# A gated attention and feed-forward kernel: the first loads cut into smaller pieces, and the instruction order made anew

## The chip, the cores and the metric

The kernel runs on one core of a Trainium2 chip. The metric is the time of the whole launch on the device in microseconds (us). The median of three runs of the kernel before is 235.07 us, the lowest 234.68 and the highest 235.65. Lower is better.

## The reference, cut to what matters

One input `x` of 2048 tokens by 512 features goes through two branches, and a gate per token mixes them:

```
g = sigmoid((x * gate_w).sum(-1))
qkv = x @ wqkv                         # 32 heads of 16
scores = q @ k.T * 16**-0.5            # key within the last 256 tokens, causal
a = (softmax(scores) @ v) @ wo
b = (silu(x @ w1) * (x @ w3)) @ w2     # 512 -> 1376 -> 512
out = g * a + (1 - g) * b
```

All inputs and the output are bf16. TensorE accumulates in f32.

## The kernel before, in words

Everything stays in SBUF. The tokens are worked on in four chunks of 512 (called `tq` in the attention branch and `tcb` in the feed-forward branch), and the heads in four groups of eight (called `c`). `xT` holds x transposed, features on the partitions. Its first chunk is made on TensorE: `load_x` (line 394) brings rows of x into `xs`, four tiles of 128 tokens; line 493 transposes each tile with four matmuls against the identity; lines 498 (VectorE) and 500 (ScalarE, tile 2 only) copy the result into `xT`. The other three chunks are made by DMA transposes, four for each chunk (`turn_x`, line 399).

Work on TensorE, by line of the profile: 420 is warm-up, matmuls of constants that nothing reads; 493 is the transposes; 553 is the products for q and k, 606 the ones for v; 661 (main) and 711 (edge) are the scores; 801 is the mix of the probabilities with v; 904 is a few columns left over by the feed-forward branch and the gate; 967 is the products with w1 and w3 for a block `f` of 128 hidden columns; 1026 and 1082 are the products with w2; 1055 is the product with wo. Line 665 and line 715 on ScalarE are the exponentials of the scores (60 main and 16 edge groups). Lines 977, 981 and 987 make the hidden block from the products of line 967.

Three forms of matmul use the array differently. Most products use all 128 rows and 128 columns ("full"). The scores use 32 rows at a time, four matmuls beside each other ("row"). The mix of line 801 uses 17 columns at a time, four beside each other ("column").

The order is made by a planner in the kernel itself, run when the program is built. `add` notes an operation with its engine, a duration, what it depends on, and a due time; `Plan.emit` is a list scheduler that goes through a model of the engines and picks, among the operations that could start, the one with the earliest due time. It charges 0.108 us (`SWITCH`) where TensorE goes from one form to another. Each engine then runs its instructions in exactly that order, and waits at one that is not ready. Due times come from formulas with the constants of the dictionary `K`, plus a correction for each operation out of the list `SHIFT` (1518 numbers). Two constants weigh forms: `ADJ` makes a score or mix group more urgent when TensorE is already out of the full form, `SEP` moves the due time of a mix group when it is in the full form. The list `landed` tells the planner when loads arrive.

`opening()` runs ahead of the planner's order: constants on GpSimd, `warm_up(WARM)` on TensorE, and then the loads, in the order written, on the queues of SyncE (SP) and ScalarE (ACT). `load_w(..., True)` splits a load of weights into two halves of the contraction, one on each queue; without `True` it goes on SP alone. The loads on SP after the first columns of w1 are: the first columns of k's weights, of w3, of q's weights, of v's weights, then the middle columns of w1 and of w3 (line 406 all of them), then the DMA transposes of the second chunk (line 399), with the remaining columns of w1 and w3 and the transposes of the third chunk behind them.

For the first chunk the first products don't wait for all of x: the block `f = 0` with w1, and q and k, are made in two halves of 256 tokens, so that the first half needs x tiles 0 and 1 only. In the block `f = 1` the four matmuls have 512 tokens each, and in the planner's model they wait for the block before them, its product with w3 included (`last_up`).

Of the kernel before, what the change touches and what calls it, by code (L numbers as in the profile page):

```python
# [21 lines left out]
    0, 0, 0, 0, 0, 0, 0, 0, 0, 0, 0, 0, 0, 0, 0, 0, 0, 143.67, 103.37, 60.03, 88, 142.21, 38.94, 42.12, -2.51, 57.41,  # L22
    7.18, 5.57, 21.6, 47.86, 56.17, 15.18, 29.67, -86.47, 13.05, -39.24, 93.68, 44.01, 89.92, -46.77, -6.15, 204.82,
    244.36, 118.35, -0.3, 95.3, 208.67, 25.01, 209.9, 27.11, 36.54, -10.95, -9.39, 52.09, 0.17, 72.67, 71.83, 128.25,
    6.95, 43.72, 49, 19.26, 15.62, -14.34, -2.54, -2.99, -55.81, 62.72, 81.66, -59.72, 182.92, 1.14, 47.94, -51.05,
    34.34, 120.64, -10.49, -37.49, -6.12, 109.58, 7.32, 0.8, 2.54, 4.2, -2.85, -45.95, -9.51, -2.95, -20.63, 0.64,
    1.17, 35.64, 39.39, 131.17, 8.36, 8.93, 28.12, 5.47, 64.98, 117.35, 1.82, 6.71, 27.65, -126.55, -12.59, -19.75,
    3.38, -14.15, 36.7, 31.02, 55.28, -21.94, 5.71, -3.9, 18.93, 47.83, 4.25, 248.79, -3.85, 44.01, 54.86, -56.69,
    127.59, -36.08, 122.73, 149.98, 17.63, -69.18, 35.62, 91.79, 17.07, 187.88, 62.3, -10.76, 56.83, 74.21, 98.54,
    100.73, -24.69, -15.4, -41.78, -18.37, 109.81, -34.23, 179.41, 88.53, 19.81, -33.97, 126.03, 79.32, 23.61,  # L30
    -111.17, 187.19, 73.42, -15.39, -4.02, 168.01, -6.39, 2.63, -49.27, -6.51, -21.07, -10.37, 98.77, -31.22, 26.94,
    -14.53, -25.32, -4.69, 10.73, -3.69, -10.22, -23.5, 6.07, 21.26, -12.87, -9.95, 66.48, 12.55, 19.01, -14.97,
    -12.27, 17.42, -5.66, 54.92, -7.76, 5.66, 29.85, 3.41, -8.01, 102.45, 40.82, 70.9, 23.07, 49.07, -36.02, 39.67,
    -10.85, -93.98, -13.12, -39.31, -4.37, 22.32, 105.78, -4.03, -8.06, -27.45, 9.46, 252.7, 20.84, -42.23, 96.29,
    107.25, -16.6, 28.68, -10.33, -22.99, 40.24, 29.98, 93.7, -5.71, 5.47, 151, 208.74, 26.61, -42.84, 51.17, -52.39,
    104.04, 21.6, 119.61, 49.37, 6.4, 83.87, 72.92, -18.55, 258.45, 169.05, 39.53, 6.4, 30.89, 29.41, 36.06, -22.79,
    40.5, 30.01, 194.39, 106.93, 198.49, 59.17, 15.42, -22.13, 31.91, -121.23, -43.1, -47.51, 37.94, 50.7, 26.07,
    -32.38, 33.8, 28.69, 14.17, 9.66, -86.66, -8.77, 15.07, 50.34, -64.11, -3.44, 7.45, -67.78, 110.17, -63.05,
    -178.58, 2.13, 121.36, -21.41, -44.26, 16.75, -37.15, -40.61, -95.25, -94.71, -87.05, -24.61, 13.42, -59.78,
    -67.44, 41.44, -101.56, 11.06, -33.11, -71.21, -28.85, 104.6, 24.33, -40.69, -52.39, -9.63, 26.77, -100.79,  # L40
    -90.72, -16.71, -49.95, 0.77, 56.94, 31.08, 2.94, 85.99, -47.92, -4.21, -10.14, -49.68, -59.14, -20.47, 17.05,
    9.18, -136.81, -17.89, -31.18, -53.9, -51.12, -31.87, -117.82, -45.29, -37.28, -12.19, -1.25, 41.48, -13.15,
    -2.78, -20.58, 70.46, -9.65, 0.42, -7.8, 138.5, 3.14, -40.82, -3.62, -15.69, -66.41, -68.61, 48.26, 0.27, -16.69,
    -84.28, 9.7, 64.3, 5.27, -19.71, -2.32, 46.57, -29.07, 2.28, -87.36, -30.22, -9.39, 9.35, -12.6, 137.81, -7.54,
    -44.64, -15.97, -33.95, 39.77, -67.24, -102.54, -33.51, 16.97, 33.23, -20.98, 103.26, -74.1, -20.35, -129.81,
    -11.87, 70.04, -37.92, -31.23, -31.72, 115.18, -5.02, 7.08, -36.32, -89.83, 69.39, -21.91, -127.54, -91.99, 58.96,
    47.44, 24.28, -21.24, -24.84, 6.43, -17.59, 13.95, 53.11, -173.96, -3.2, 2.87, 76.58, -23.35, 0.24, 44.93, 6.77,
    32.61, -43.31, -3.8, 54.69, 32.74, 20.67, -11.12, -7.84, -5.91, 113.99, 8.97, 31.35, 9.04, -33.31, -70.77, 125.18,
    -11.8, 13.25, 41.86, -23.6, 32.12, -117.51, -69.74, 4.45, 3.22, -45.12, -13.56, 7.83, -1.49, -61.88, -17.3,
    -30.07, 81.28, 54.45, 60.43, 3.73, 8.99, -19.3, -55.65, -126.93, 28.33, -26.47, -99.46, -105.24, -53.49, -36.19,  # L50
    -105.94, -6.28, -8.53, 9.04, -131.6, -67.07, -32.86, -0.62, -26.8, -15.17, 42.29, -25.61, 0.66, -115.05, 8.73,
    -156.43, -126.84, -74.33, -116.11, -42.3, 106.05, -83.79, -84.91, -56.93, -39.89, 40.69, -58.82, -16.3, -68.75,
    -113.67, -46.33, -55.59, 86.72, -2.31, -4.54, -147.15, -65.61, -56.93, -9.05, -63.33, -74.13, -51.4, -43.18,
    -165.22, -18.68, 28, 28.73, -49.15, -97.68, -110.31, -7.88, -19.74, 90.28, -107.22, 10.84, -11.65, -12.48,
    -139.53, 101.05, 15.07, 40.93, -29.49, -17.58, -11.49, -93.56, -20.27, -15.93, 1.59, -20.21, -55.65, -25.66,
    -13.61, -2.96, 15.71, -29.74, -54.27, -59.15, -10.64, -38.16, -50.35, 98.06, 69.37, -37.63, -5.15, -141.83,
    165.05, -222.91, 67.89, -61.75, -90.82, 86.05, 60.99, -103.98, -18.7, 43.14, 47.89, -10.91, -25.67, -47.43, 11.14,
    8.9, 37.39, -55.89, -46.72, -5.35, 19.74, -95.65, -21.88, -53.61, -8.14, -32.99, -73.67, -20.88, 10.04, -67.08,
    143.23, 72.28, 2.19, 196.98, -84.67, -76.21, -83.98, 32.86, -106.11, -80.37, -10.73, 2.47, -154.03, -73.23, 83.93,
    4.83, -11.7, 18.76, 4.53, -5.17, -169.97, -86.68, 36.64, 7.28, -109.75, -129.22, 9.09, -37.03, -73.61, -50.85,  # L60
    -82.09, 34.51, -83.71, -84.57, -105.55, -51.2, -28.08, -96.33, 16.35, -21.62, -35.06, -64.78, 140.85, -38.85,
    -76.38, -48.32, 0.11, -136.54, -65.55, -85.88, -68.18, -1.47, -19.95, -104.98, 3.42, -38.57, -97.15, -46.27,
    27.73, 19.45, -81.04, -136.13, -59.96, -160.69, -114.6, -45.93, 209.18, 10.81, -66.32, -51.02, -128.13, 16.41,
    -129.46, -42.8, 69.77, -11.72, -85.17, -0.02, 13.79, 51.92, -164.37, -35.41, -17.3, 107.06, -55.49, -146.53,
    13.95, -10.84, -8.11, -173.24, -84.51, 51.45, -6.56, -9.72, -138.28, -139.48, -56.4, -80.09, -20.29, -124.07,
    -28.97, -198.75, -2.49, 31.49, -109.38, 49.16, -19.84, -90.85, -183.08, 86.7, -11.55, 75.95, -47.51, -13.11,
    -143.48, -132.62, -156.14, -139.7, -162.81, -118.44, 35.58, -10.76, -13.59, -122.48, -167.03, -145.19, -108.13,
    1.53, -98.19, -90.01, -124.36, 4.22, -3.94, -76.47, 44.12, 1.73, -108.31, -4.23, -120.54, 3.35, -9.5, 1.03, -2.62,
    5.39, -177.73, -56.91, -103.65, -64.6, -98.27, -76.43, -36.83, -179.23, -130.6, -147.17, 84.55, -107.32, 11.46,
    -3.2, -25.91, 22.58, -171, -129.24, -77.58, 13.67, 4.85, -93.34, -179.61, -36.75, 1.36, 26.22, -125.29, -138.89,  # L70
    -153.86, 5.16, -51.58, -76.87, -154.65, 16.68, -60.17, 17.84, -81.88, -0.77, -11.98, -199.53, -3.2, 24.53,
    -122.57, -80.18, -107.59, 21.59, 22.98, -80.5, -145.36, -152.67, 31.99, -91.15, -114.97, 76.44, 30.12, -168.03,
    -152.87, -62.63, -31.09, -23.28, 1.02, 10.23, 23.56, -68.32, -141.82, -74.89, -41.69, 2.78, -111.71, -179.08,
    19.29, -12.38, -129.45, -108.99, -87.66, -25.52, -79.85, 86.01, -135.14, 135.58, -177.44, -51.77, -30.02, -113.8,
    40.25, 16.46, -216.88, -6.71, 16.72, 10.99, 0.28, 36.46, 16.66, 21.49, 86.9, -7.91, -4.28, -35.85, 116.8, 116.67,
    -6.87, 31.59, -21.27, 46.82, -51.08, -6.69, -18.61, 1.49, 62.93, 119.51, 65.71, -24.1, 3.72, -24.61, -20.61,
    -63.52, 73.67, 28.77, 35.06, 50.97, -44.06, 2.71, -54.72, -37.79, -0.52, 55.39, -42.49, -33.84, -34.29, -35.32,
    5.43, 14.68, 19.8, -12.27, 83.28, 73.04, 16.23, -39.95, 12.12, -46.08, 10.28, -22.12, 11.92, 209.9, 5, 0.32,
    66.04, -19.2, 12.74, -42.84, 22.8, 5.12, 159.56, 0.64, 41.85, -25.48, 72.07, 125.81, 95.22, 36.82, 36.62, 10.6,
# [183 lines left out]
def kernel(  # L263
# [12 lines left out]
    nc = tc.nc  # L276
# [17 lines left out]
    VW = DH + 1  # L294
    HALF = (0, 1, 2, 3, 4)
    SCALE = float(DH) ** -0.5
    WARM = 30

    pp = ctx.enter_context(tc.tile_pool(name="pp", bufs=1))
    ps = ctx.enter_context(tc.tile_pool(name="ps", bufs=1, space=bass.MemoryType.PSUM))  # L300
# [148 lines left out]
    T0, TA, TF0, TF1 = K["T0"], K["TA"], K["TF0"], K["TF1"]  # L449
# [684 lines left out]
```

## Time and profile before

| what | value |
|---|---|
| median of 3 runs | 235.07 us (234.68 to 235.65) |
| the profiled execution's own time | 235.33 us |
| its span, first to last instruction | 233.6 us |
| PE (TensorE) busy | 225.2 us, 96% of the span |
| ScalarE, VectorE, GpSimd busy | 181.9, 181.7, 152.8 us |
| read from HBM, written | 6.85 MB, 2.10 MB |

The profiled execution took 1.7 us more than its span, which is what lies before the first and after the last instruction. Busy time of PE is not PE at its peak: the durations of matmuls overlap, so the stretches in which the array streams nothing are found from the starts of the instructions, not from the busy share.

### The profile page before, as it was taken

To read this page: it belongs to the slowest core of one execution; us is meant where nothing else is said; L and a number is where in the kernel's file an instruction comes from. 1 tells how busy PE (TensorE), PEld (TensorE's weight loads), DVE (VectorE), ACT (ScalarE), POOL (GpSimd) and SP (SyncE) were. 2 spreads that over 40 slices of the span, in tenths; PEclk is the share of its full clock that TensorE was granted. 3 is DMA by queue.
4 is the path that set the end of the run, shared out by engine and by line. 5 is a ranking of instruction groups with operands and counts; after the bars stand their busy time and mean duration, and the time that the engine had idled before them with its cause. 6 is when DMAs were issued, how large, how long until landed. Compare 5 with 4: busy or idle time off the path is not lost.

```text
span 233.6 us, 8254 instructions
## 1 busy us (share of the span) xinstructions
PE 225.2 (96%) x3596; PEld 115.9 (50%) x3635; DVE 181.7 (78%) x317; ACT 181.9 (78%) x165; POOL 152.8 (65%) x245
## 2 busy tenths in 40 slices
PE   7999999999999999999999999999999999999995
PEld 7545545634544345545547353535444355455543
DVE  5457777993798869987878787887986779997864
ACT  3479999797778998878998989887968998867310
POOL 7135999576877964749865869567679856654300
DMA  6997701800004000000003000000000000140202
GB/s 188 322 183 196 93 1 21 225 27 1 6 4 133 3 11 14 3 3 3 4 12 81 25 1 3 3 3 0 4 3 3 0 3 18 34 145 20 91 7 84
DMA packets 20653, 11.57 MB, mean 50 GB/s; under 512 B 10025, under 2 KB 20617, under 8 KB 20617
## 3 DMA queue, kind: packets, MB, share of 16 engines
q1 hardware_dynamic: 19920, 10.62, 19.5%
q8 instruction: 28, 0.46, 0.8%
q10 hardware_dynamic: 696, 0.43, 0.6%
q14 instruction: 9, 0.07, 0.1%
HBM read 6.85 MB, written 2.10 MB: 38 GB/s over the span
## 4 chain that ended last, share of the span: by engine, by line
PE 89%; DMA 4%; SPq 2%; issue 2%; DVE 2%
PE ch L967 30%; PE ch L1026 16%; PE ch L553 11%; PE ch L801 9%; PE su L661 8%; PE ch L606 6%; PE ch L1055 6%; PE su L711 2%; DMA xT<-in_A_x_dram 2%; SPq L399 2%; DMA xs<-in_A_x_dram 2%; PE ch L1082 1%; PE ch L904 1%; SPq L406 1%; DVE bsb L1030 0%
## 5 line engine op out<-in xcount | busy, mean ns | idle before, releaser
L665 ACT ACTIVATE Em<-su 128x2048 bf16<-128x2048 f32 x60 | 112.7, 1878 | 22.5 <-PE su L661 20.9
L967 PE MATMUL ch<-xT,w_sb 128*128 128x512 bf16 (+1 forms) x304 | 77.0, 377 | 2.7 <-issue 1.7
L675 POOL TENSOR_SCALAR_AFFINE_SELECT Em<-Em 64x512 bf16<-64x512 bf16 x56 | 37.8, 674 | 26.2 <-ACT Em L665 24.5
L670 POOL TENSOR_SCALAR_AFFINE_SELECT Em<-Em 64x512 bf16<-64x512 bf16 x60 | 40.5, 676 | 18.0 <-ACT Em L665 16.0
L728 POOL TENSOR_SCALAR_AFFINE_SELECT Ee<-Ee 64x1024 bf16<-64x1024 bf16 x32 | 39.5, 1233 | 11.4 <-ACT Ee L715 10.3
L967 PEld LDWEIGHTS <-w_sb 128*128 128x128 bf16 x324 | 28.7, 98 | 32.8 <-issue 4.7
L981 DVE SCALAR_TENSOR_TENSOR h<-tt,ch 128x512 bf16<-128x512 bf16 (+1 forms) x44 | 29.7, 679 | 12.9 <-ACT tt L977 12.6
L1026 PE MATMUL ch<-w_sb,hT 128*128 128x512 bf16 x143 | 37.0, 380 | 0.8 <-issue 0.6
L553 PE MATMUL ch<-xT,wqkv_sb 128*128 128x512 bf16 (+1 forms) x126 | 33.5, 367 | 0.6 <-issue 0.3
L715 ACT ACTIVATE Ee<-su 128x2048 bf16<-128x2048 f32 x16 | 30.1, 1880 | 5.0 <-PE su L711 5.0
L642 POOL COPY vs<-vs 64x256 bf16<-64x256 bf16 x64 | 28.9, 452 | 7.5 <-DVE vs L630 3.1
L987 DVE SCALAR_TENSOR_TENSOR hT<-h,ch 128x512 bf16<-128x512 bf16 x40 | 27.1, 682 | 5.4 <-PE ch L967 3.3
L977 ACT ACTIVATE tt<-ch 128x512 bf16<-128x512 f32 (+1 forms) x44 | 26.1, 598 | 3.9 <-PE ch L967 3.1
L801 PEld LDWEIGHTS <-vs 128*17 128x17 bf16 x1664 | 20.5, 92 | 5.8 <-issue 4.5
L801 PE MATMUL ch<-Em,vs 128*17 128x256 bf16 (+2 forms) x672 | 22.6, 242 | 0.0
L801 PE MATMUL ch<-Ee,vs 128*17 128x64 bf16 x992 | 22.1, 193 | 0.0
L1026 PEld LDWEIGHTS <-hT 128*128 128x128 bf16 x150 | 13.5, 98 | 16.4 <-issue 2.5
L553 PEld LDWEIGHTS <-wqkv_sb 128*128 128x128 bf16 x136 | 12.0, 97 | 13.3 <-issue 2.7
L606 PE MATMUL ch<-wqkv_sb,xT 128*128 128x256 bf16 x128 | 17.2, 273 | 0.2 <-issue 0.2
L661 PE MATMUL su<-qT,kz 32*128 32x256 bf16 x240 | 17.3, 278 | 0.0
L661 PE MATMUL su<-qT,k 32*128 32x256 bf16 x240 | 16.6, 268 | 0.0
L661 PEld LDWEIGHTS <-kz 32*128 32x128 bf16 x240 | 6.0, 91 | 21.2 <-issue 20.8
(83 smaller groups left out, 251.9 us busy)
## 6 DMA issues: line engine op xcount, KB each, us to landing
out_dram<-ot SPq DMA_DIRECT2D x15, 128.0 KB, 1.7
wqkv_sb<-in_A_wqkv_dram SPq DMA_DIRECT2D x6, 256.0 KB, 4.5
w_sb<-in_B_w_dram SPq DMA_DIRECT2D x2, 608.0 KB, 4.8
w_sb<-in_B_w_dram SPq DMA_DIRECT2D x3, 384.0 KB, 3.8
w_sb<-in_B_w_dram SPq DMA_DIRECT2D x2, 512.0 KB, 6.5
wo_sb<-in_A_wo_dram SPq DMA_DIRECT2D x4, 128.0 KB, 3.2
xs<-in_A_x_dram ACTq DMA_DIRECT2D x1, 256.0 KB, 3.8
xs<-in_A_x_dram SPq DMA_DIRECT2D x1, 256.0 KB, 3.5
```

The lines of the kernel that those rows point to most:

```text
L553: nc.tensor.matmul(pst[:, t0:t1], lhsT=wqkv_sb[:, dc, col + c * P:col + (c + 1) * P], rhs=xT[:, dc, tq * 512 + t0:tq * 512 + t1], start=(d ...
L606: nc.tensor.matmul(ch[vj.at["ch"]][:, (m - m0) * 2 * P:(m - m0 + 1) * 2 * P], lhsT=xT[:, dc, m * P:(m + 1) * P], rhs=wqkv_sb[:, dc, 2 * D ...
L661: nc.tensor.matmul(su[:, s, a * 256:(a + 1) * 256], lhsT=head_keys(r, t, a), rhs=qT[r, q0:q0 + 256], start=True, stop=True)
L665: nc.scalar.activation(out=Em[job.at["Em"]][:], in_=su[:].rearrange("p s (a q) -> p s a q", a=2), func=ACT.Exp, scale=SCALE)
L670: nc.gpsimd.affine_select(out=e, in_=e, pattern=[[0, 8], [1, KB]], compare_op=ALU.is_ge, fill=0.0, base=0, channel_multiplier=-1)
L675: nc.gpsimd.affine_select(out=e, in_=e, pattern=[[0, 8], [-1, KB]], compare_op=ALU.is_ge, fill=0.0, base=-1, channel_multiplier=1)
L715: nc.scalar.activation(out=Ee[ej.at["Ee"]][:].rearrange("p s t k q -> p s (t k q)"), in_=su[:], func=ACT.Exp, scale=SCALE)
L728: nc.gpsimd.affine_select(out=e, in_=e, pattern=[[0, 4], [0, 4], [1, KB]], compare_op=ALU.is_ge, fill=0.0, base=0, channel_multiplier=-1)
L801: nc.tensor.matmul(po[32 * s:32 * s + VW, lo - 512 * w:hi - 512 * w], lhsT=vs[:, i, a * VW:(a + 1) * VW], rhs=mov, start=(n == 0), stop=(n ...
L967: nc.tensor.matmul(ch[job.at["ch"]][:, t0:t1], lhsT=wA[:, dc, :] if joint else w[:, dc, f * P:(f + 1) * P], rhs=xT[:, dc, tcb * 512 + t0:t ...
L981: nc.vector.scalar_tensor_tensor(out=h1[job.at["h1"]][ru, :], in0=tt[job.at["tt"]][rg, :], scalar=1.0, in1=ch[job.at["ch"]][rg, :], op0=AL ...
L1026: nc.tensor.matmul(bps[:], lhsT=ht[:, mm * P:(mm + 1) * P], rhs=w2_sb[0:fs, f, :], start=(f == 0), stop=(f == NFC - 1))
```

## The change

The loads of x are cut from two pieces of 256 KB into four of 128 KB, one for each tile of 128 tokens. Tiles 0 and 1 go first, one on each queue; then come the two halves of w1's first columns; then tiles 2 and 3. The warm-up has 23 matmuls where it had 30. For the first chunk the product of w1 with block `f = 1` is made in two halves of 256 tokens, as block `f = 0` was already, and the planner no longer makes it wait for `last_up`. `landed` has new arrival times for x and for w1's first columns. The constants `K` are new, and so are all numbers of `SHIFT` (now 1516, since two operations are gone); with them the order of the whole program is a new one. The numbers of `SHIFT` are cut here to the first line of each list.

```diff
 SHIFT = [
-    0, 0, 0, 0, 0, 0, 0, 0, 0, 0, 0, 0, 0, 0, 0, 0, 0, 143.67, 103.37, 60.03, 88, 142.21, 38.94, 42.12, -2.51, 57.41,
...
+    0, 0, 0, 0, 0, 0, 0, 0, 0, 0, 0, 0, 0, 0, 0, 0, 0, 4.69, -2.58, -20.58, -2.83, 1.06, 0.72, 24.53, 0.21, 7.18,
...
 ]
-    WARM = 30
+    WARM = 23
-    K = {"T0": 1.021, "TA": 175.674, "TF0": -5.614, "TF1": 219.201, "PV": -22.302, "EDGE": -2.04, "HOLD": -6.16, "LEAD": -1.713, "QLEAD": -2.523, "V": 9.16, "O0": 9.293, "O1": -5.39, "O2": 6.658, "O3": 32.037, "FE": 0.855, "PE": 8.645, "VE": -2.133, "MK": 65.837, "UP": 4.276, "_km": 1.0, "_lo": 1.0, "LE": 1.877, "ADJ": 7.677, "SEP": -19.643, "BE": 5.555, "OE": 1.299, "END": 5.842}
+    K = {"T0": 2.227, "TA": 175.361, "TF0": -4.255, "TF1": 213.877, "PV": -6.113, "EDGE": 0.732, "HOLD": -0.443, "LEAD": 0.942, "QLEAD": -5.414, "V": 7.151, "O0": 14.885, "O1": 5.66, "O2": 8.135, "O3": 27.069, "FE": 2.213, "PE": 8.461, "VE": -3.49, "MK": 40.302, "UP": 6.634, "_km": 1.0, "_lo": 1.0, "LE": -1.709, "ADJ": 2.616, "SEP": -4.351, "BE": 8.777, "OE": 3.124, "END": 7.045}
@@ opening()
         warm_up(WARM)
 
-        load_x(0, 2, nc.sync)
-        load_x(2, 4, nc.scalar)
+        load_x(0, 1, nc.sync)
+        load_x(1, 2, nc.scalar)
         load_w(w1_sb, B_w1, 0, 2 * P, True)
+        load_x(2, 3, nc.sync)
+        load_x(3, 4, nc.scalar)
         nc.scalar.activation(out=gt[:, 0:4], in_=nc.const_aps.tensor_like(1.0, gt[:, 0:4]), func=ACT.Tanh)
         nc.scalar.dma_start(out=gwr[:], in_=gate_w.rearrange("(c p) -> c p", p=P))
         load_w(wqkv_sb, A_wqkv, D, D + 2 * P)
@@ arrivals
-    landed = {"x": [3.6, 3.6, 4.4, 4.4, 14.5, 20.6], "w13": [5.25, 7.45, 10.8, 16.6, 12.2, 18.8],
+    landed = {"x": [3.25, 3.6, 5.4, 5.6, 14.5, 20.8], "w13": [4.8, 7.45, 10.8, 16.6, 12.2, 18.8],
               "qkv": [6.5, 8.3, 9.1], "gw": 8.0}
@@ feed-forward, block f of chunk tcb
-            if tcb or f:
+            if tcb or f > 1:
                 a = plan.pieces(HALF, 0.2155, lambda lo, hi, half=half, job=job: half(job, w1_sb, lo, hi),
                                 xt_ready[tcb] + win + last_up + (w_ab if joint else []), due, [(job, "ch")])
             else:
                 (two halves of 256 tokens, the second behind x tiles 2 and 3)
```

## The prediction

> **What bounds the kernel now.** I read the page first, then the busy time by stretches.
>
> ```profile
> PE 225.2 (96%) x3596; PEld 115.9 (50%) x3635; DVE 181.7 (78%) x317; ACT 181.9 (78%) x165; POOL 152.8 (65%) x245
> PE 89%; DMA 4%; SPq 2%; issue 2%; DVE 2%
> 18.00:70.00 52.00, 51.10 (x873) 26.81 (x885) 40.18 (x71) 43.95 (x42) 40.25 (x67) 1.00 0.27 62
> ...
> 180.00:225.00 45.00, 44.31 (x770) 21.65 (x776) 38.14 (x63) 31.66 (x27) 24.96 (x32) 1.00 0.13 40
> ```
>
> TensorE (PE) is the bound: 89% of the chain that ended last is its work, and from 18 to 225 us it idles about 1 us in 50. The other engines have a fifth of their time free. So a change to the order can help in three ways only: by an earlier start of dense PE work, by less PE time that streams nothing, or by a shorter tail. The tail first, out of the chain of waits:
>
> ```profile
> 228.96 1.84 PE ch L1082 x22
> 230.82 0.35 DVE ot L1086
> ```
>
> After the last matmul (230.79) come one eviction and one store, to 233.6: 2.8 us that no edit touches but the order. I take 0 for it.
>
> Which PE time streams nothing? The chain of waits, in two places, and the counts of score groups on the page:
>
> ```profile
> 17.42 0.65 PE ch L553 x3
> 18.07 0.33 PE su L661 x8
> 18.40 0.32 PE ch L553
> ...
> 36.70 0.33 PE su L661 x8
> 37.03 1.12 PE ch L801 x80
> 38.15 0.32 PE ch L967
> ...
> 208.44 1.46 PE ch L801 x112
> 209.90 0.33 PE su L661 x8
> L665 ACT ACTIVATE Em<-su 128x2048 bf16<-128x2048 f32 x60 | 112.7, 1878 | 22.5 <-PE su L661 20.9
> L715 ACT ACTIVATE Ee<-su 128x2048 bf16<-128x2048 f32 x16 | 30.1, 1880 | 5.0 <-PE su L711 5.0
> ```
>
> A matmul of 512 columns takes 0.65 / 3 = 0.216 us in a row of its kind; after a score group the next takes 0.32. So each change of form, into the score form or out of it, costs 0.32 - 0.216 = about 0.11 us. There are 60 + 16 = 76 score groups and, counted along PE's order, 17 mix groups (line 801). Each alone between full matmuls would mean 2 x 93 = 186 changes. Where a mix group touches a score group, one change is saved. That is so in 14 places (the first at 36.70, the last at 209.90), so there are 172 changes, 172 x 0.11 = 18.9 us. This is the one large item that a new order can move.
>
> **The opening, as it stands.** Engine by engine in order of time, PE alone:
>
> ```profile
> 0.85 3.17 PE L420 MATMUL su<-const-bfloat16-1.0 128*128 128x128 bf16 x30 [0.85 <-PEq L1118]
> 4.34 0.62 PE L493 MATMUL ch<-ident,xs 128*128 128x128 bf16 x8 [0.31 <-DMA xs<-in_A_x_dram]
> 4.91 0.61 PE L493 MATMUL ch<-ident,xs 128*128 128x128 bf16 x8
> 5.58 1.07 PE L967 MATMUL ch<-xT,w_sb 128*128 128x256 bf16 x8
> 6.80 1.04 PE L553 MATMUL ch<-xT,wqkv_sb 128*128 128x256 bf16 x8 [0.15 <-issue]
> 15.31 1.03 PE L553 MATMUL ch<-xT,wqkv_sb 128*128 128x512 bf16 x3
> ```
>
> and the durations of single instructions by line (shortest, median, longest in ns), the third of the lines from 4 to 8 us:
>
> ```profile
> L420 PE MATMUL su<-const-bfloat16-1.0 x32: 219/311/311, 0.9 to 4.9; 128*128 128x128 bf16 x32
> L493 PE MATMUL ch<-ident,xs x16: 217/219/229, 4.3 to 5.3; 128*128 128x128 bf16 x16
> L967 PE MATMUL ch<-xT,w_sb x10: 270/272/379, 5.6 to 7.9; 128*128 128x256 bf16 x8, 128*128 128x512 bf16 x2
> ```
>
> Useful PE work begins at 4.34 with the transposes. Real products begin at 5.58. The eight half-width matmuls from 5.58 take 1.07 - 0.27 (the last one's own duration) over seven steps, 0.11 each, so they stream until 5.58 + 8 x 0.11 = 6.46; the next work waits for k's weights and starts at 6.80: a hole of 0.34. At 15.31 three matmuls of 0.216 spread over 1.03 where 2 x 0.216 + 0.38 (the duration at 512 columns) = 0.81 would do: a wait of 0.22 for a DMA transpose of the second chunk.
>
> How x gets in: GB/s is the last column of the busy time by stretches, and the landings are in the DMA view.
>
> ```profile
> 2.00:2.50 0.50, 0.50 (x7) 0.50 (x6) 0.33 (x2) 0.50 (x1) 0.50 (x4) 1.00 0.98 98
> 2.50:3.00 0.50, 0.50 (x8) 0.50 (x6) 0.50 (x1) 0.50 (x1) 0.40 (x3) 1.00 0.79 217
> 3.00:3.50 0.50, 0.50 (x8) 0.50 (x6) 0.42 (x4) 0.37 (x2) 0.39 (x3) 1.00 1.04 360
> 3.50:4.00 0.50, 0.50 (x7) 0.35 (x5) 0.12 (x1) 0.00 (x0) 0.45 (x3) 1.00 1.09 373
> xs<-in_A_x_dram ACTq DMA_DIRECT2D x1, 256.0 KB, 3.8
> xs<-in_A_x_dram SPq DMA_DIRECT2D x1, 256.0 KB, 3.5
> w_sb<-in_B_w_dram SPq DMA_DIRECT2D x1, 128.0 KB, 3.9
> ```
>
> Summed, the rows give 49 + 109 + 180 + 187 = 525 KB by 4.0, the 512 KB of x. They land at 0.82 + 3.5 = 4.3 (SP) and 0.81 + 3.8 = 4.6 (ACT), so 0.3 to 0.6 after their last bytes moved.
>
> **The change, part by part.**
> 1. *x in four pieces.* The first two tiles are the first 256 KB, which by these rows have moved at 3.0 + 99 / 360 = 3.27; with the same lag they land between 3.6 and 3.9. I take 3.75, 0.6 ahead of 4.34. From the first transpose to the first half product it took 5.58 - 4.34 = 1.24 (transposes, then two copies one behind the other on VectorE), so that product can start at 3.75 + 1.24 = 5.0. w1's halves are the next 256 KB; they move by 4.0 and land by 4.6, not later. Dense work begins 0.58 earlier: **-0.58**.
> 2. *The transposes of tiles 2 and 3* ran before that start; now they run inside the dense stretch: 8 matmuls of 0.056 (0.61 less one duration of 0.22, over 7 steps) = **+0.45**.
> 3. *Block 1 in halves, free of the block before:* 8 x 0.11 for 4 x 0.216, so +0.01. It gives PE 0.87 us of work that needs w1 and x alone; this fills the hole before k's weights: **-0.34**. What is late next is tiles 2 and 3: they come behind 512 KB, so they can't land before w1 did (1.34 + 3.9 = 5.2). Transposed and copied (1.24 again) they give xT at 6.5. The two first halves of blocks 0 and 1 cover PE to 5.0 + 0.87 + 0.45 = 6.3, and k's first half, with its weights landed before 6.80, the rest.
> 4. *Seven warm-up matmuls fewer:* (3.17 - 0.22) / 29 = 0.10 each on the mean, so the row ends near 0.85 + 3.17 - 0.7 = 3.3 instead of 4.02. They are ahead of everything useful, so 0 by themselves, if PE's clock doesn't mind (a rival, below).
> 5. *The queues.* SP's own waits and the chain of waits in the opening:
>
> ```profile
> SPq L406 <- DMA xs<-in_A_x_dram: 1.2, 1, 1.2
> 0.81 3.83 DMA xs<-in_A_x_dram
> 4.66 0.37 SPq L406
> 5.07 0.56 SPq L406
> 5.68 0.69 SPq L406
> 6.42 1.58 SPq L399
> ...
> 10.52 5.40 DMA xT<-in_A_x_dram
> ```
>
> SP issues five loads and ACT three, and the ninth stands until a piece of x has landed (4.64). From there SP issues without a pause, and the second chunk arrives at the end of this very chain (10.52 + 5.40 = 15.92), where PE waits the 0.22 seen above. With two more loads ahead, the ninth is no longer v's weights but w3's first columns, with q's behind them. It waits for a first piece of x, at 3.6 to 4.0; then w3, q, v and two loads of columns have to be issued (0.5 + 0.5 + 0.37 + 0.56 + 0.69 and five pauses of 0.04 = 2.8) before the first DMA transpose: at 6.4 to 6.8, or 7.0 if v's must wait for w1's landing. So the second chunk comes 0 to 0.6 late. If its products stand at the same place in PE's order, the wait of 0.22 grows by that; if work is put ahead of them, by nothing. I take **+0.15**. w3's columns themselves, issued 1.7 us later, land at 4.0 + 3.8 (the time of an x piece from an empty queue) = 7.8 at the latest, where 7.68 is when PE used them; block 1 covers that.
>
> Opening: -0.58 + 0.45 + 0.01 - 0.34 + 0.15 = **-0.3**, with ends at -0.6 (queue harmless, no copy late) and +0.5 (x 0.3 later than I think, chunk two 0.6 late).
>
> 6. *The order made anew.* No row shows it. The ends come from the changes of form: all 34 sides of the 17 mix groups beside a score group, 20 more than now, would give 20 x 0.11 = -2.2; none would give 14 x 0.11 = +1.5. In the constants, `SEP` no longer hurries a mix group by 19.6 us out of the full form but by 4.4, and `ADJ` rewards closeness with 2.6 instead of 7.7. Out of the full form a mix group was 12 us more urgent than beside a score group; now the two differ by 1.7. That leans to more closeness, but `SHIFT` can outweigh it anywhere. I stay with the present count, **0**.
>
> Sum: the profiled execution took 235.33, 0.26 over the median. 235.33 - 0.3 = 235.0 in such an execution, and 235.07 - 0.3 = **234.8** as a median.
>
> **The rivals.**
> *A better order.* Twelve more places where mix and score groups touch, 12 x 0.11 = 1.3, besides the opening: 235.07 - 1.6 = 233.5. For it: 20 such places are still open, and the due times lean that way. Against: nothing in the profile says that they can be had at once with full buffers.
>
> *The clock (ends slower).* The last of the warm-up, in PE's order of time:
>
> ```profile
> 3.69 0.34 PE L420 MATMUL su<-const-bfloat16-1.0 128*128 128x128 bf16 x3
> ```
>
> These three are (0.34 - 0.22) / 2 = 0.06 apart, where the row as a whole has 0.10, and by the durations above most warm-ups take 311 ns, the transposes of the same shape 219. So PE starts at half speed and steps up near 3.7, after 2.84 us of unbroken matmuls since 0.85. With 23 the row ends at 3.3, and then PE has some 0.45 us of work until 5.0. If the step hasn't come by then and the count starts anew with the products at 5.0, they run at half speed for 2.84 us and lose 1.42: 235.07 - 0.3 + 1.4 = 236.2. It decides where the step falls after 3.3. Against it: waits for w1 and k's weights in that stretch would hide a part, and PE is not idle for long. The Trainium skill (TensorE: Matmul & The Clock Gate, Part 1: The HAM clock gate) says that the clock doubles after a busy window of about 3.4 us, and that the window runs freely, not from the kernel's start; the trace's 2.84 us agrees with a window that began earlier. By that rule a missed window would cost 3.4 / 2 = 1.7, an estimate from the page, and only in some executions.
>
> *A worse order.* All 14 touching places gone, +1.5, with an opening at its slow end of +0.2: 236.8. For it: an order is a point in a large space, and PE has only 1 us in 50 to lose, so a wait in the wrong place shows in full. Against: the formulas lean the other way.
>
> *The pieces land no earlier,* because the lag of 0.3 to 0.6 is the piece's and not the queue's: x at 4.2, products at 5.45, and the opening is +0.1: 235.2.
>
> **How the numbers follow.** Chances: forecast 0.32, better order 0.30, worse order 0.19, clock 0.12, no earlier landing 0.07. A difference of 0.5% (1.2 us) is about what a measurement can tell from none. Faster: 0.30 + 0.03 from the forecast's own spread = 0.33. Slower: 0.19, half of the clock's, 0.03 from the forecast = 0.28. Within: 0.39. The range of 8 in 10 goes from 233.0 (some beyond the better order) to 237.0 (the worse order with little more); the forecast's own is 234.0 to 235.7.
>
> **What would show it right or wrong.** Transposes (line 493) starting by 3.9 and the first product (line 967) by 5.1, no hole before line 553; SP's first DMA transpose between 6.4 and 7.0; the first products of line 553 on the second chunk at 15.9 to 16.6; places where lines 661 or 711 touch line 801 counted against 14; warm-ups at 311 ns followed by products at 273 and not at double. I am wrong if PE, once dense, shows waits above 1 us in sum, or if its last matmul does not move with the sum of these terms.

## The result and the profile after

| what | before | after |
|---|---|---|
| median of six runs on one chip | 235.3 us (234.68 to 235.65) | 236.45 us (235.67 to 236.94) |
| ratio after / before, 95% interval | | 1.0049 [1.0025, 1.0073] |
| the profiled execution's own time | 235.33 us | 235.67 us |
| its span | 233.6 us | 234.0 us |
| half products with w1 start | 5.58 us | 5.20 us |

The changed kernel is slower by about 1.15 us, where 0.3 less was forecast: the direction is wrong. The profiled execution is the shortest of its six, 0.8 below their median, so its trace can explain 0.3 of the loss and not the rest. That rest needs other executions, and they come below. One execution of one of those kernels took 289.65 us at a granted clock of 0.75; it is in no ratio, but in the median of 237.48 that the expectation for that kernel's second run names.

Up to the loads, line numbers are 15 lower than before: 405 is the warm-up, 379 the loads of x, 391 the loads of weights, 384 the DMA transposes. Behind the loads they are 13 lower: 480 is the transposes, 485 the copies to `xT`, 954 the products with w1 and w3, 540 those for q and k, 593 for v, 648 and 698 the scores, 788 the mix, 1013, 1042 and 1069 the late products. The experiments' kernels have other lengths again: with two or three pieces of x these lines are 2 or 1 lower, and where the order is written out as a list, 447 or 449 is the transposes, 921 or 923 the products with w1 and w3, and 507 or 509 those for q and k.

The page after, busy times and the chain that ended last:

```profile
PE 229.4 (98%) x3632; PEld 116.0 (50%) x3632; DVE 181.6 (78%) x317; ACT 182.0 (78%) x165; POOL 151.8 (65%) x245
PE 94%; DVE 3%; DMA 1%; issue 0%
```

TensorE is the bound as before. Its 229.4 against 225.2 us is no added work: the changed program has 3 matmuls fewer (7 warm-ups less, 4 more for the halves of block 1), and yet before's trace has 3596 and after's 3632, so some 39 of before's records are missing. Starts can be compared; busy sums can't, and a gap between two records of before may be a product whose record is missing.

The opening after, PE in order of time (start, duration of the stretch, line, operation, count, and in brackets the idle time ahead and what ended it):

```profile
0.85 2.61 PE L405 MATMUL su<-const-bfloat16-1.0 128*128 128x128 bf16 x23 [0.85 <-PEq L1105]
3.65 1.03 PE L480 MATMUL ch<-ident,xs 128*128 128x128 bf16 x8 [0.19 <-DMA xs<-in_A_x_dram]
...
5.20 1.05 PE L954 MATMUL ch<-xT,w_sb 128*128 128x256 bf16 x8 [0.30 <-DVE xT L485]
6.08 0.61 PE L480 MATMUL ch<-ident,xs 128*128 128x128 bf16 x8
6.98 0.60 PE L540 MATMUL ch<-xT,wqkv_sb 128*128 128x256 bf16 x4 [0.29 <-DVE xT L485]
```

The first tiles land at 3.6 and are transposed at once, but the eight transposes take 1.03 us where before's took 0.62: at 3.65 PE's clock is still at half. The half products start at 5.20. Behind them come the transposes of tiles 2 and 3, and then a new hole, 6.52 to 6.98. The chain of waits says what PE stood for (start, duration, what):

```profile
6.24 0.24 PE ch L480 x4
6.48 0.02 issue
6.50 0.44 DVE xT L485
6.94 0.04 issue
6.98 0.60 PE ch L540 x4
...
14.65 0.32 PE ch L954
14.97 1.06 PE ch L540 x4
```

VectorE's copy of tile 3 holds up the first half of k, which needs tiles 0 and 1 only and had those since 5.16. What it can lack is a PSUM bank: the two open halves and the two transposed tiles hold the four banks of `ch`. But k's weights came hardly earlier. TensorE's loading of weights into the array, PEld in the profile, had to wait for them as well:

```profile
6.82 0.48 PEld L540 LDWEIGHTS <-wqkv_sb 128*128 128x128 bf16 x4 [0.30 <-DMA wqkv_sb<-in_A_wqkv_dram]
```

So with a bank free at once, a hole from 6.52 to about 6.85 would have stayed. At 14.97 four matmuls take 1.06 where 4 x 0.216 = 0.86 would do: 0.20 of waiting for the second chunk.

Later the chain shows two waits that before did not have, and the tail:

```profile
170.93 0.58 PE ch L1013 x2
...
215.13 0.65 DVE ot L1046
...
215.82 0.38 PE ch L1042
...
229.87 1.25 PE ch L1069 x22
...
231.14 0.35 DVE ot L1073
```

Two matmuls in 0.58 where 0.43 would do, and 0.22 for an eviction at 215.6. The last matmul ends at 231.12, before's at 230.82 (its last row, 228.96 + 1.84, in the prediction).

**How large the hole was before.** The prediction reads a hole of 0.34 ahead of k, from 6.46 to 6.80, and most of it was work. PEld loads weights for nine products there, where PE's records have eight (the row at 6.80). The kernel before with 33 warm-ups, whose trace lacks no record, shows the ninth: the first of the row has 512 columns, and takes 0.216. In order, PEld in before, then PE with 33 warm-ups:

```profile
6.57 0.98 PEld L553 LDWEIGHTS <-wqkv_sb 128*128 128x128 bf16 x9 [0.20 <-DMA wqkv_sb<-in_A_wqkv_dram]
```

```profile
7.35 1.25 PE L553 MATMUL ch<-xT,wqkv_sb 128*128 128x512 bf16 x9
```

So in before PE streamed from 6.80 - 0.216 = 6.59 on, right behind the loading of k's weights at 6.57, and idled 0.10 from 6.49.

**Where the 0.3 went, from the starts on PE.** The half products start 0.38 earlier. The transposes of tiles 2 and 3 stand behind them now: +0.45. The hole ahead of k is 0.45 where it was 0.10: +0.35. Two waits of before inside the first 16 us, 0.26 for w3's middle columns and 0.22 for the second chunk, have become 0.20: -0.28. The first of them, in before's PE rows, is nine matmuls of 0.216 that take 2.38 where 2.11 would do, and PEld shows what the last two waited for:

```profile
11.35 2.38 PE L967 MATMUL ch<-xT,w_sb 128*128 128x512 bf16 x9
```

```profile
13.12 0.11 PEld L967 LDWEIGHTS <-w_sb 128*128 128x128 bf16 x2 [0.59 <-DMA w_sb<-in_B_w_dram]
```

From 16 us on there are one change of form more, +0.11, and the two waits above, +0.37. Together that is +0.6, and the last matmul ends only 0.30 later; the other 0.3 is not placed, and the records missing from before's trace are where smaller waits of before could hide. Counted along PE, mix and score groups touch in 11 places of 16 + 76 groups: 2 x 92 - 11 = 173 changes against 172.

### The profile page after: what moved, and what is told of

Read it like the earlier page. It is cut to its first block, busy times and chain, and to the rows that moved or that the text cites. A ratio compares the mean times of both kernels' runs of the same rounds, so it can differ in the third digit from the quotient of the medians.

```text
span 234.0 us, 8293 instructions
## 1 busy us (share of the span) xinstructions
PE 229.4 (98%) x3632; PEld 116.0 (50%) x3632; DVE 181.6 (78%) x317; ACT 182.0 (78%) x165; POOL 151.8 (65%) x245
## 3 DMA queue, kind: packets, MB, share of 16 engines
HBM read 6.85 MB, written 2.10 MB: 38 GB/s over the span
## 4 chain that ended last, share of the span: by engine, by line
PE 94%; DVE 3%; DMA 1%; issue 0%
PE ch L954 33%; PE ch L1013 15%; PE ch L540 13%; PE ch L788 9%; PE su L648 8%; PE ch L593 6%; PE ch L1042 5%; PE su L698 2%; DMA xs<-in_A_x_dram 1%; PE ch L891 1%; DVE xs L828 1%; DVE xT L485 1%; PE ch L1069 1%; DVE nt L834 0%; PE ch L480 0%
## 5 line engine op out<-in xcount | busy, mean ns | idle before, releaser
L954 PE MATMUL ch<-xT,w_sb 128*128 128x512 bf16 (+1 forms) x328 | 81.3, 375 | 0.3 <-DVE xT L485 0.3
L662 POOL TENSOR_SCALAR_AFFINE_SELECT Em<-Em 64x512 bf16<-64x512 bf16 x56 | 37.0, 661 | 23.5 <-ACT Em L652 21.8
L657 POOL TENSOR_SCALAR_AFFINE_SELECT Em<-Em 64x512 bf16<-64x512 bf16 x60 | 40.1, 669 | 18.4 <-ACT Em L652 16.3
L954 PEld LDWEIGHTS <-w_sb 128*128 128x128 bf16 x328 | 29.9, 98 | 34.3 <-issue 5.3
L1013 PE MATMUL ch<-w_sb,hT 128*128 128x512 bf16 x150 | 38.7, 380 | 0.0
L540 PE MATMUL ch<-xT,wqkv_sb 128*128 128x512 bf16 (+1 forms) x136 | 36.5, 368 | 0.3 <-DVE xT L485 0.3
L1017 DVE TENSOR_SCALAR bsb<-ch,omg 128x512 bf16<-128x512 f32 x15 | 11.2, 745 | 6.9 <-PE ch L1013 6.8
```

Source lines behind the costliest of these rows:

```text
L540: nc.tensor.matmul(pst[:, t0:t1], lhsT=wqkv_sb[:, dc, col + c * P:col + (c + 1) * P], rhs=xT[:, dc, tq * 512 + t0:tq * 512 + t1], start=(d ...
L657: nc.gpsimd.affine_select(out=e, in_=e, pattern=[[0, 8], [1, KB]], compare_op=ALU.is_ge, fill=0.0, base=0, channel_multiplier=-1)
L662: nc.gpsimd.affine_select(out=e, in_=e, pattern=[[0, 8], [-1, KB]], compare_op=ALU.is_ge, fill=0.0, base=-1, channel_multiplier=1)
L954: nc.tensor.matmul(ch[job.at["ch"]][:, t0:t1], lhsT=wA[:, dc, :] if joint else w[:, dc, f * P:(f + 1) * P], rhs=xT[:, dc, tcb * 512 + t0:t ...
L1013: nc.tensor.matmul(bps[:], lhsT=ht[:, mm * P:(mm + 1) * P], rhs=w2_sb[0:fs, f, :], start=(f == 0), stop=(f == NFC - 1))
```

## The experiments

Every ratio is against runs of the kernel before on the same chip. The order is the planner's own unless the text says that it is written out as a list; what is computed is the same in all. n is the number of runs behind a median.

### Once more, and the warm-up

The changed kernel unchanged; the changed kernel with before's 30 warm-up matmuls; the kernel before with the change's 23.

```diff
 after, 30 warm-ups
-    WARM = 23
+    WARM = 30
 before, 23 warm-ups
-    WARM = 30
+    WARM = 23
```

> The changed kernel once more, to see its spread beside the others on one chip. Its profiled execution took 235.67 us, the shortest of six; the median was 236.45. Clock theory (the shorter warm-up lets PE's step to full speed come late in most executions): median near 236.4, spread over 1 us, and another profiled execution may show half-speed products behind line 954's start at 5.2. Order theory (the new order and opening cost the same in every execution): spread as in the kernel before, products at full speed from 5.2.

> The changed kernel with 30 warm-up matmuls again. Clock theory: 0.6 to 0.9 us less than the changed kernel, so about 235.7, and a narrower spread. Order theory: no gain, 236.4, or 0.1 to 0.2 more, since the warm-up now ends after x's first tile has landed.

> The kernel before with 23 warm-up matmuls, nothing else changed. Clock theory: 0.5 to 1.0 us more than the kernel before, since x lands at 4.3 here and PE idles from 3.3 on. Order theory: no change within 0.2 us.

| kernel | median us (range, n) | ratio |
|---|---|---|
| changed, again | 236.13 (235.45 to 237.93, 12) | 1.0030 [1.0011, 1.0049] |
| changed, 30 warm-ups | 236.16 (235.76 to 236.97, 12) | 1.0029 [1.0015, 1.0042] |
| before, 23 warm-ups | 236.46 (235.30 to 237.46, 12) | 1.0035 [1.0017, 1.0053] |

The profiled execution of the changed kernel, run again, took 237.16. PE's rows of that execution:

```profile
3.69 1.03 PE L480 MATMUL ch<-ident,xs 128*128 128x128 bf16 x8 [0.22 <-DMA xs<-in_A_x_dram]
...
5.24 1.87 PE L954 MATMUL ch<-xT,w_sb 128*128 128x256 bf16 x8 [0.30 <-DVE xT L485]
6.90 1.06 PE L480 MATMUL ch<-ident,xs 128*128 128x128 bf16 x8
8.05 1.01 PE L540 MATMUL ch<-xT,wqkv_sb 128*128 128x256 bf16 x4
```

Same order, same loads, but eight half products take 1.87 instead of 1.05 and four of k 1.01 instead of 0.60: PE runs at half speed until 9.2. This is the rival "the clock", and its span is 1.4 longer than in the first trace, the price that the prediction gave it. That the price agrees is in part chance: half speed lasted 4.0 us from the first product on and not 2.84, and shorter waits (none for the second chunk) took some of it back. It happens in some executions; that the spread of the twelve runs, 2.5 us, is mostly that is a guess from two traces.

With 30 warm-ups the spread is half of that (1.2 us), as the clock theory had it, and the median does not move, as the order theory had it. Its trace suggests why. PE and then SyncE's queue:

```profile
5.20 1.03 PE L954 MATMUL ch<-xT,w_sb 128*128 128x256 bf16 x8 [0.51 <-DVE xT L485]
...
14.90 1.05 PE L540 MATMUL ch<-xT,wqkv_sb 128*128 128x512 bf16 x3
16.11 0.38 PE L540 MATMUL ch<-xT,wqkv_sb 128*128 128x512 bf16 x1 [0.16 <-DMA xT<-in_A_x_dram]
```

```profile
6.79 5.91 SPq L384 DMA_TRANSPOSE xT<-in_A_x_dram  x4
```

The clock is full from 3.9 on, and PE arrives at the second chunk before the chunk does: the four matmuls start at 14.90 and end at 16.48, 1.58 where 1.02 would do, so 0.56 are waits. What the earlier clock gave, the queue took, in this execution. The queue was late because of x: the load ahead of the DMA transposes waited for the last piece of x, which landed at 6.1 here and at 5.76 in the first trace. In the kernel before, cutting the warm-up cost 0.0035 x 235.4 = 0.8 us; in the changed one nothing that these runs show. The cut is a loss by itself, but in this kernel it doesn't explain the median.

### The pieces of x

With 30 warm-ups and the new order kept, x in two pieces as before, and in three (tiles 2 and 3 as one, behind w1).

```diff
 two pieces
-        load_x(0, 1, nc.sync)
-        load_x(1, 2, nc.scalar)
+        load_x(0, 2, nc.sync)
+        load_x(2, 4, nc.scalar)
         load_w(w1_sb, B_w1, 0, 2 * P, True)
-        load_x(2, 3, nc.sync)
-        load_x(3, 4, nc.scalar)
 three pieces
-        load_x(2, 3, nc.sync)
-        load_x(3, 4, nc.scalar)
+        load_x(2, 4, nc.scalar)
```

> The changed kernel with 30 warm-up matmuls and x in two pieces again, the new order kept. It leaves only the new order and block 1 in halves. If the pieces bring the 0.4 us by which products started earlier in the trace (5.20 for 5.58): 0.4 us more than the one with 30 warm-ups and four pieces. If the pieces bring nothing that lasts: the same time.

> The changed kernel with 30 warm-ups and x in three pieces: tiles 0 and 1 as in the change, tiles 2 and 3 in one load on ACT, so one load fewer stands ahead of SP's waiting loads. With four pieces and 30 warm-ups the products started at 5.20 and PE then waited 0.56 us for the second chunk's DMA transposes at 15.1 to 15.8; with two pieces they started at 5.64 and PE waited nothing there; both took the same time. Issue theory (the extra loads hold up SP's queue, each later load waits for the landing of the one eight before it): first DMA transpose issued 0.3 to 0.5 us earlier than with four pieces, the wait falls under 0.25, 0.3 to 0.4 us less time than with four pieces, about 235.8. Bytes theory (the data itself comes late): no change, 236.2.

Two pieces: 235.99 (235.60 to 236.41, 12), 1.0029 [1.0016, 1.0042], the same ratio as four. Its PE rows and its first DMA transposes:

```profile
5.64 1.10 PE L952 MATMUL ch<-xT,w_sb 128*128 128x256 bf16 x8 [0.30 <-DVE xT L483]
6.58 0.61 PE L478 MATMUL ch<-ident,xs 128*128 128x128 bf16 x8
7.48 0.60 PE L538 MATMUL ch<-xT,wqkv_sb 128*128 128x256 bf16 x4 [0.29 <-DVE xT L483]
...
15.30 1.03 PE L538 MATMUL ch<-xT,wqkv_sb 128*128 128x512 bf16 x4
```

```profile
6.36 5.62 SPq L384 DMA_TRANSPOSE xT<-in_A_x_dram  x4
```

The four pieces start the products 0.44 earlier (5.20 against 5.64; a part of that is the clock, since with two pieces the transposes ahead ran at half speed in the profiled execution); two pieces start them later and have no wait at 15.3, where four matmuls take their plain 1.03, against 0.56 of waits. By the end the difference is nearly gone. By the medians the pieces themselves neither pay nor cost; in these two executions what they win at 5 us is handed back at 15.

Three pieces: 236.34 (236.03 to 237.10, 8), 1.0045 [1.0026, 1.0063]. The expectation that one load fewer lets the DMA transposes start sooner missed. SyncE's queue:

```profile
4.62 2.57 SPq L391 DMA_DIRECT2D w_sb<-in_B_w_dram  x2
7.24 5.69 SPq L384 DMA_TRANSPOSE xT<-in_A_x_dram  x4
```

They start at 7.24, later than with four pieces. The piece of 256 KB that ends x lands at 7.1, and the queue goes on right behind it. From the ninth on, each load's record carries a wait for a semaphore that an earlier load raises when it lands; eight are used in turn (in the changed kernel the ninth names that of x's first piece). So a load waits for the landing of one some eight before it, by the program's own semaphores; whether the chip's queue has a limit besides is not shown. Which load lands late counts, and not how many there are. In this execution the clock rose only at 6.4 to 6.8 as well.

### The transposes of tiles 2 and 3

Two pieces, 30 warm-ups, the new order written out as a list, with one thing in it moved: the transposes of tiles 2 and 3 and their copies go ahead of the first products, and the second halves right behind the first. On PE that gives 16 transposes, 16 half products with w1, then k and q.

```diff
 PE's part of the order, first chunk
-  transposes 0, 1; first halves of blocks 0, 1; transposes 2, 3; first half of k; second halves of blocks 0, 1; ...
+  transposes 0, 1, 2, 3; first and second halves of blocks 0, 1; first half of k; ...
```

> The changed kernel's order with x in two pieces and 30 warm-ups, and in the opening the transposes of tiles 2 and 3 ahead of the first products, as in the kernel before; then the four halves of blocks 0 and 1 without a break, then k. Compared with two pieces and the order of the change it takes 0.45 us of transposes and a wait of 0.45 out of the dense stretch. If PE alone sets the opening: 0.9 us less, 235.1. If the second chunk's arrival sets it: the gain is given back in waits before 16 us as soon as PE gets there early, 0.4 to 0.6 us remain, 235.4 to 235.6.

235.44 (235.21 to 236.56, 12), 1.0006 [0.9990, 1.0021]. Against 1.0029 for the same kernel with the new order's own opening, that is 0.0023 x 235.4 = 0.54 us, as the second of the two expectations had it. The two intervals overlap a little (1.0016 to 1.0021), and the traces below say where the time went. PE's rows:

```profile
5.07 0.61 PE L447 MATMUL ch<-ident,xs 128*128 128x128 bf16 x8
5.63 1.91 PE L921 MATMUL ch<-xT,w_sb 128*128 128x256 bf16 x16
7.38 1.91 PE L507 MATMUL ch<-xT,wqkv_sb 128*128 128x256 bf16 x16
...
14.34 1.41 PE L507 MATMUL ch<-xT,wqkv_sb 128*128 128x512 bf16 x4
```

and its chain of waits:

```profile
10.77 4.56 DMA xT<-in_A_x_dram
...
15.37 0.38 PE ch L507
```

The products start at 5.63, as in before, and nothing interrupts them: no transposes in between, and no hole, since the copies run under the half products. That takes 0.45 + 0.45 = 0.9 us out. PE reaches the second chunk at 14.34, one microsecond ahead of the 15.30 of the other, and waits there: 1.41 where 1.02 would do, 0.39 given back. The remainder agrees with the measured 0.54. And since this kernel keeps the whole new order after 8 us and stands at 1.0006, the new order behind the opening is worth nothing that these runs can tell, somewhere from -0.2 to +0.5 us by the interval.

### The second chunk's transposes ahead in the queue

Four pieces, 30 warm-ups, the planner's own new order; the second chunk's DMA transposes go ahead of w3's middle columns on SyncE.

```diff
         load_w(w1_sb, B_w1, 2 * P, 6 * P)
+        turn_x(1)
         load_w(w3_sb, B_w3, 2 * P, 6 * P)
-        turn_x(1)
```

> The changed kernel (four pieces) with 30 warm-ups, and in SP's queue the DMA transposes of the second chunk ahead of the middle columns of w3, which PE uses first at about 18 us. With 30 warm-ups alone PE waited 0.56 us for those transposes (15.1 to 15.8), and the kernel took 236.16. If the earlier start of the products was lost in that wait: chunk two lands about 1 us earlier, no wait there, 0.4 to 0.5 us less, 235.7. If the wait was only a symptom and PE loses the same time elsewhere: no change within 0.15.

235.86 (235.68 to 236.41, 12), 1.0012 [1.0000, 1.0024]; with the old queue it was 1.0029. PE and the queue:

```profile
5.07 1.08 PE L954 MATMUL ch<-xT,w_sb 128*128 128x256 bf16 x8 [0.51 <-DVE xT L485]
...
15.00 1.03 PE L540 MATMUL ch<-xT,wqkv_sb 128*128 128x512 bf16 x4
```

```profile
6.25 5.15 SPq L384 DMA_TRANSPOSE xT<-in_A_x_dram  x4
```

The wait at 15 is gone, and 0.4 us of time with it. The two intervals overlap, so the ratio alone would not carry this; the trace adds that PE reached the second chunk 0.10 later than with the old queue (15.00 for 14.90), lost none of the 0.56 there, and ended 0.46 earlier. By this pair the start at 5 us pays when the queue keeps up.

### The old order with the new opening

Four pieces, 30 warm-ups, before's order written out, with only the opening's steps taken from the change: blocks 0 and 1 in first halves, then tiles 2 and 3, half of k, the second halves.

```diff
 PE's part of the order
-  the change's order
+  before's order; in front of it: transposes 0, 1; first halves of blocks 0, 1; transposes 2, 3; first half of k; second halves; second half of k
```

> The opening of the change with 30 warm-ups (four pieces, blocks 0 and 1 in halves ahead of the transposes of tiles 2 and 3), and behind it the order of the kernel before, written out as a list. Opening theory (what the change costs lies before 16 us): 0.6 to 0.7 us over the kernel before, the same as the changed kernel with 30 warm-ups. Order theory (part of the cost is the order behind it: one change of form more, waits at 171 and 216 us): 0.3 to 0.4 us less than that kernel, about 0.3 over the kernel before.

> The opening of the change in front of the order of the kernel before, once more for a profile: it took 237.48 in the median, 1.3 more than with the new order, and its profiled execution ran at a clock of 0.75. Join theory (the old order behind the new opening waits for banks of PSUM or data before 20 us): waits of 1 us or more in PE before 20 us, none above 0.3 behind. Late theory: waits spread over the rest.

The first run gave 237.43 (236.71 to 237.67, 5), 1.0085 [1.0063, 1.0108], and no trace to compare. Run again: 237.35 (237.23 to 237.53, 3), 1.0076 [1.0052, 1.0101]. The first expectation, +0.3, missed by 1.5 to 1.7 us. PE's rows:

```profile
6.80 0.62 PE L449 MATMUL ch<-ident,xs 128*128 128x128 bf16 x8 [0.56 <-DMA xs<-in_A_x_dram]
...
11.84 0.59 PE L509 MATMUL ch<-xT,wqkv_sb 128*128 128x512 bf16 x2 [0.22 <-DVE h L937]
```

and the waits of PE over the whole execution (who waited, for what: sum, times, longest):

```profile
PE ch L449 <- DMA xs<-in_A_x_dram: 0.6, 1, 0.6
PE ch L923 <- DVE xT L454: 0.5, 1, 0.5
PE ch L509 <- DVE vs L586: 0.4, 1, 0.4
```

Here a tile of x landed at 6.75, not 5.8; PE's waits for it, for the copies behind it and for buffers add up to 1.8 us before 13, as the join theory had it; one of 0.57 follows at 63.6, where that theory had none above 0.3. So the order did have to be made anew for this opening: before's order around the new pieces costs 0.0047 x 235.4 = 1.1 us more than the new one (1.0076 against 1.0029 with 30 warm-ups). How much of the 1.8 is the late tile, which no order makes, one trace can't say.

### A longer warm-up before, and all repairs together

```diff
 before, 33 warm-ups
-    WARM = 30
+    WARM = 33
 all repairs: the kernel with tiles 2 and 3 transposed first, and
         load_w(w1_sb, B_w1, 2 * P, 6 * P)
+        turn_x(1)
         load_w(w3_sb, B_w3, 2 * P, 6 * P)
-        turn_x(1)
 ...and in the written order one score group ahead of the matmul that waits at 215
```

> The kernel before with 33 warm-ups, which fill PE's wait for x (4.0 to 4.3). Clock theory: the step to full speed comes more surely before the products; 0.1 to 0.3 us less in the median and a narrower spread. If 30 are enough: no change within 0.1.

> x in two pieces, 30 warm-ups, transposes of all four tiles ahead of the four halves of blocks 0 and 1 (which alone took 235.44), and besides: the second chunk's DMA transposes ahead of w3's middle columns, and one score group moved ahead of a matmul that waited 0.22 us for VectorE at 215. Its waits were 0.39 at 14.8 to 15.1 and 0.22 at 215. If both go: 0.4 to 0.6 us less, 234.9, 0.2% under the kernel before. If the chunk's landing is not what PE waits for: 235.2.

Before with 33: 235.79 (234.69 to 236.20, 12), 1.0017 [1.0003, 1.0032], slower where a gain was expected. Its profiled execution has matmuls without a break from 0.85 on, and still:

```profile
4.32 1.06 PE L493 MATMUL ch<-ident,xs 128*128 128x128 bf16 x8
...
5.39 0.99 PE L493 MATMUL ch<-ident,xs 128*128 128x128 bf16 x8
6.22 1.29 PE L967 MATMUL ch<-xT,w_sb 128*128 128x256 bf16 x8
```

Transposes of 1.06 and 0.99, where full speed gives 0.61: the clock rose at about 6.1. Three more warm-ups were no remedy.

All repairs: 235.32 (234.77 to 236.38, 12) against 235.64 for before on that chip, 0.9994 [0.9978, 1.0010]. The wait at 215 is gone from its chain, and the one at 15 too, though PE also came 0.8 later to the second chunk than without the last two repairs. Expected were 0.4 to 0.6 us less than without them; the ratios differ by 0.0012, 0.3 us, within the noise. It has the lowest ratio of the kernels here and can't be told from the one before; no version that beats both is shown.

## Why the prediction went wrong, by its own steps

**Step 1, the earlier start: -0.58 forecast, -0.38 in the trace.** The tiles landed as told (3.60 for 3.75). The 1.24 from the first transpose to the first product became 1.55, because the transposes ran at half speed; with 30 warm-ups, where they ran at full speed, it was 1.23 (3.97 to 5.20). The same 1.24 was read off an execution whose clock had just risen, and was carried to an earlier moment where it hadn't.

**Step 2, the transposes inside: +0.45, right** (0.61 less one duration, as forecast).

**Step 3, the hole: -0.34 forecast, +0.35 found. This step failed, in three places.** First, the term was mis-sized: before's hole was 0.10, and 0.22 of the 0.34 was a product whose record the trace lacks. Second, the weights: by the prediction's own figures the work put into the hole ended at 6.3 and k's weights came "before 6.80", so it could not all be filled. They were issued on SP behind one more piece of x (at 2.24, before at 1.84) and went into the array from 6.82 on (before from 6.57); the prediction moved w3's, q's and v's weights for the longer queue, and left k's where they were. Third, a buffer: the prediction asked for weights and tokens and not for a PSUM bank. Tiles 2 and 3 landed at 5.45 and 5.76 (later than the 5.2 given as the earliest), and k stood until the copy that ends at 6.94. With x in two and in three pieces k's first weights were in the array 0.51 before k started (6.97 and 7.48, 7.55 and 8.06), and the hole was 0.45 all the same: there it is the copy alone that k waits for. That the copy counts because it frees a bank is read from the kernel; no run gave it a fifth bank. What was shown is that without the interleaving both the hole and the transposes of step 2 go from the dense stretch, for 0.54 net.

**Step 4, seven fewer warm-ups: 0 by themselves.** They let the transposes start at 3.65 rather than 3.97 (30 warm-ups end there), and the half-speed clock took that back: products at 5.20 with either. In the kernel before, the cut costs 0.8 us.

**Step 5, the queue: +0.15, ends 0 to 0.6.** The first DMA transpose came at 6.58 in the first trace, inside the 6.4 to 7.0 given. In that trace the wait was 0.20 for 0.22, no growth. In the one with 30 warm-ups it was 0.56, and there moving the transposes ahead in the queue brought 0.4. The place of the second chunk's products, forecast for 15.9 to 16.6, was 14.8: the new order asks for the chunk earlier, and that is what makes the queue matter.

**Step 6, the order: 0, ends -2.2 to +1.5.** Right in size behind the opening: 173 changes for 172, two new waits of 0.15 and 0.22, and a whole of 1.0006 for the kernel that has the new order but not its opening. What the order does cost, 0.54 with 30 warm-ups and two pieces of x, lies in the first 8 us. The measured 236.45 comes near the rival of a worse order (236.8), but not by its mechanism: that had all 14 touching places gone, and 11 are there. The better order, with 12 such places more, falls too.

**The clock**, given 0.12, is real in single executions (1.4 us in the second trace) and shows in the spread. It does not show in the median of the changed kernel, 1.0030 with 23 and 1.0029 with 30 warm-ups, perhaps because PE that comes later waits less for the second chunk; the traces show each side of that trade, but how often each occurs was not measured. The Trainium skill (TensorE: Matmul & The Clock Gate, Part 1: The HAM clock gate) puts the rise after a busy window of about 3.4 us, running freely and so varying by about 0.5 us. The traces agree that it varies without the kernel's doing, and not on the size: the rise fell anywhere from 3.6 to 9.2 us.

**No hole before k, and waits.** Of the signs named, the transposes (3.65) and the queue held, the first product missed by 0.1, and the hole and the second chunk's place were wrong. Dense PE's waits, the hole included, come to 1.0 us (0.45, 0.20, 0.15, 0.22), at the bound named, and the other sign of being wrong came: the last matmul moved by +0.30, and not by the sum of the terms.

What stays open: how the loss of the median, 0.7 us by the second measurement and 1.15 by the first, divides between clock, hole and queue, since one execution shows one clock; why the last tile of x lands at 5.76 in one execution and 6.75 in another; and what sets the moment of the clock's rise.

## What to carry to other kernels

A step that is moved into dense work must be asked three things, not two: are its data there, are its weights there, and is a buffer free for its result. Before a gap is counted as one to be filled, the records around it must be counted: a trace can lack some, and weight loads (PEld) beside the products, or another trace of the same order, show it. A start won at the beginning is only won if the next thing that PE will wait for, here the second chunk behind a longer queue, comes earlier by as much; check that queue in the same edit. A duration read from a stage where the clock has just risen doesn't hold for the same work 0.7 us earlier.

## What the runs showed of the hardware

The rise of PE's clock to full speed, read from the spacing of matmuls in twelve profiled executions, fell between 3.6 and 9.2 us after the span's start, though PE began at 0.85 in all. With 30 warm-ups it came from 3.6 to 6.8, with 23 from 4.6 to 9.2, with 33 at 6.1; the changed kernel gave 4.6 to 5.2 in one execution and 9.2 in another. The clock column of the profile doesn't show it: it reads 1.00 in that second execution from 5 to 9 us, where products of 256 columns stand 0.21 apart instead of 0.11. A late rise need not show in the time: the profiled execution of the kernel before with 23 warm-ups, the fastest of its twelve, had it at 6.5, and yet the span of the one with 30 and a rise at 3.7, 233.6 us both. Its PE rows:

```profile
6.00 1.34 PE L967 MATMUL ch<-xT,w_sb 128*128 128x256 bf16 x8
7.39 1.04 PE L553 MATMUL ch<-xT,wqkv_sb 128*128 128x256 bf16 x8
...
15.62 0.81 PE L553 MATMUL ch<-xT,wqkv_sb 128*128 128x512 bf16 x3
```

The products of k start 0.6 later than in the first trace of before (6.80), those on the second chunk 0.3 later (15.31), and these take 0.81 instead of 1.03: before's waits for w3's middle columns and for the chunk, 0.26 and 0.22, took up the rest.
